# A fused attention and feed-forward kernel with its 522 operations in a new order

## The chip, the cores and the metric

The kernel runs on one core of a Trainium2 chip. A core has five engines with an instruction queue each: TensorE (PE in the profile; PEld is its weight load), VectorE (DVE), ScalarE (ACT), GpSimd (POOL) and SyncE (SP), which here only issues DMA transfers. Each queue runs in order, and semaphores hold an instruction until what it reads is there. TensorE writes to PSUM, which has eight banks of 512 float32 columns on 128 partitions; GpSimd does not touch PSUM in this kernel. The metric is the time of one execution on the device, in microseconds. A change of less than about 2% cannot be told from none.

## The reference

Two blocks are computed one after the other. Sizes are 4 batches, 4 heads, 1088 tokens, 32 features per head, 8 sketch rows.

```python
def phi(x):                                   # 64 features per token
    a = np.einsum('rd,bhsd->bhsr', S1, x)
    b = np.einsum('rd,bhsd->bhsr', S2, x)
    return np.einsum('bhsi,bhsj->bhsij', a, b).reshape(*x.shape[:-1], r * r)
q_p, k_p = (phi(q), phi(k))
kv = np.einsum('bhsf,bhsd->bhfd', k_p, v)
z = np.sum(k_p, axis=2)
num = np.einsum('bhsf,bhfd->bhsd', q_p, kv)
den = np.einsum('bhsf,bhf->bhs', q_p, z)[..., None] + 1e-06
attn = num / den
# heads side by side: x has 128 features per token
xn = (x - mu) / np.sqrt(var + 1e-06) * g_ln
out = x + np.maximum(xn @ w_ch1, 0.0) @ w_ch2
```

The sketches and both weights come as float64; the kernel turns them into float32 by itself, from their bits.

## The kernel before

The whole schedule is one list of operations, `PROGRAM` (lines 824 to 908), which is written out and run from top to bottom. The framework's own scheduling is off (`tc.manual_schedule()`), so each engine's queue holds its operations in the order of this list. Semaphores are derived from what the operations read and write. An operation is a name with arguments: the engine, where there is a choice (`V` VectorE, `A` ScalarE, `G` GpSimd, `S` SyncE), the batch or token chunk, a range, and the PSUM banks.

The work goes through these steps.

- *Fills* (`fill n w z`, line 247) multiply ones by ones into bank z; nobody reads the result.
- *Unpacking of weights* (`w_ex`, `w_bits`, `w_exf`, `w_mant`, `w_low`, `w_e2`, `w_e3`, `w_add`, `w_mul`, lines 274 to 336) makes float32 out of float64 for the sketches (0), the first weight (1) and the second (2). `fold` (352) takes the mean and the gain of the normalization into the first weight; `fold_cp` copies it out of PSUM.
- *Sketches*: `s_heads`, `sk`, `sk_0`, `sk_2`, `sk_8`, `sk_d` (lines 338 to 405) build the matrices by which tokens are multiplied.
- *Keys of a batch*: `turn_g`, `turn_r` (414, 424) transpose 32 by 32 blocks on VectorE. Batch 0 uses `k_dir` (448) with `k_cp` and `k_prod0`; the others use `k_feat` (466), `k_tok` (475), `k_prod`. Then come `k_sum` (490), `k_zs`, `k_sc`, `k_sccp` for the sum over tokens, `k_val` (519) for the product with the values, and `k_vcp`, `k_spr` (534), `k_rcp`, which lay it out.
- *Queries of a batch*: batch 0 is transposed on TensorE (`turn_p` 431, `turn_c`) and multiplied by `q_dir` (554); the others use `turn_g`, `q_feat` (587), `q_tok` (596). Then `q_ac`, `q_den`, `q_rec` make the reciprocal denominator, `q_a2` and `q_prod` the features, `q_turn` (634) turns them, and `num` (648) multiplies. `num_cp` and `num_r` copy the result to `xT`, one chunk of 512 tokens per half batch. The last 64 tokens of two batches form the narrow chunks 8 and 9.
- *Feed-forward of a chunk c*: `hid z c j t0 t1` (757) makes 128 of 512 hidden features for the 128-token tiles t0 to t1, `relu` (765 on ScalarE, 767 on VectorE) takes them to `hT`, and `sec z c t` (773) multiplies tile t by the second weight. There are two `hT` tiles, used in turn by the chunks in the order 0, 1, 2, 3, 8, 4, 5, 6, 7, 9.
- *Rows of a chunk*: `row_turn` (710), `row_wr` (716) and `row_rd` (722) bring the attention result to rows through DRAM (`row_pe`, `row_cp` for chunks 8 and 9). `st_bn`, `st_ag`, `st_pow` (730 to 743) make the normalization's factor. `fin` (786) scales and adds on VectorE; `fin_a` (791) scales on ScalarE, and `fin_g` (801) adds. `store` (807) and `store_r` (817) write to DRAM.

The loads are `ld` (121) for k and q rows, `ld_v` (129), `ld_vr` (135), `ld_t` (143) and `ld_tr` (150) for q of batch 0, `ld_w` (158), `ld_s` (112) and `ld_g` (116).

The four batches are interleaved: keys of the next batches run while `hid` and `sec` of the first chunks are worked through. A bank is free for its next writer when its readers are done, so the banks in the list decide whom a product waits for.

Of the kernel before, what the change touches and what calls it, by code (L numbers as in the profile page):

```python
# [25 lines left out]
def kernel(  # L26
# [810 lines left out]
    w_add G 1 0 256; k_dir 0 6 9 1; sk_2 4; k_prod0 3 6 6 3; w_mul G 1 0 256; turn_p 3 4 8;
    k_cp A 0 6 9 1; ld_v S 0 3; turn_c A 5 8 9; k_sum 0 7; sk_d 4; k_prod G 0 6 9; turn_c A 3 4 8;
    k_zs 0 7; turn_g k 1 0 4; k_sc 0 7; fold 3 0 256; k_sccp A 0 7; q_dir 4 9 2;
    fold_cp A 3 0 256; turn_r k 1; ld_v S 0 2; w_low A 2 0 512; w_bits V 2 0 512; w_ex V 2 0 512;  # L840
    ld_t S 2 0 4; k_feat 1 4 5; q_cp A 4 9 2 0 24; ld_t S 1 0 4; fill 1 512 1; w_exf A 2 0 512;
    k_tok 1 4 5; q_ac G 0 4 9; ld S k 2 0 34; w_mant A 2 0 512; c_vpad 2; q_den 0 4 9;
    ld S q 1 0 34; k_sum 1 7; q_rec 0 4 9; fold 3 256 512; w_e2 V 2 0 512; ld_v S 1 1;
    q_a2 V 0 4 9; ld_v S 1 2; w_e3 V 2 0 512; k_val 0 0 3 6; q_prod V 0 6 9; q_prod G 0 4 6;
    k_val 0 3 6 6; k_val 0 6 9 6; turn_p 2 0 4; k_zs 1 7; k_vcp A 0 6; k_prod G 1 0 5; q_turn 4 9;
    k_sc 1 7; turn_c A 2 0 4; k_spr 0 6; fold_cp A 3 256 512; q_dir 0 4 1; k_rcp A 0 6;
    k_sccp V 1 7; turn_g k 2 0 4; num 0 4 9 4 5 2 3; q_cp A 0 4 1 0 24; q_ac G 0 0 4; turn_r k 2;
    w_add G 2 0 512; q_den 0 0 4; k_feat 2 6 7; num_cp A 0 1 4 8 2 3; num_cp V 0 0 4 8 4 5;
# [1 line left out]
    k_tok 2 6 7; row_wr S 1; num_r A 0 4 5; hid 0 1 1 0 4; relu A 1 1 3 0 4; ld S q 2 0 34;  # L850
    turn_r q 1; turn_g q 1 0 4; q_prod G 0 0 2; ld_vr S 1 0; hid 7 1 2 0 4; relu A 0 1 1 0 4;
    k_sum 2 6; q_turn 2 4; w_mul G 2 0 512; relu A 7 1 2 0 4; row_rd S 1; q_feat 1 3 4 0 1;
    ld_v S 1 0; k_zs 2 6; q_turn 0 2; hid 7 1 0 0 4; ld_v S 1 3; k_prod G 1 5 9; q_tok 1 0 3 4;
    ld_vr S 2 0; k_sc 2 6; ld_vr S 1 1; relu A 7 1 0 0 4; num 0 0 4 4 5 2 3; k_sccp V 2 6;
# [1 line left out]
    num_cp A 0 1 0 4 2 3; q_den 1 0 4; sec 0 1 2; q_rec 1 0 4; st_bn 1; q_a2 G 1 0 4;
    q_prod G 1 0 4; sec 4 1 3; st_ag 1; row_turn 0 1 2 3; q_den 1 4 9; hid 6 0 1 2 4; q_rec 1 4 9;
    hid 3 0 3 0 2; q_a2 V 1 4 9; hid 0 0 0 0 2; relu A 3 0 3 0 2; row_turn 0 0 4 5; st_pow 1;
    k_val 1 0 9 2; relu A 6 0 1 2 4; q_turn 0 4; row_wr S 0; ld S k 3 0 34; sk_qq 3; fin_a 4 1 3;
    hid 5 0 0 2 4; q_prod G 1 4 9; turn_g q 2 0 4; relu A 0 0 0 0 2; hid 4 0 1 0 2; fin_a 0 1 2;  # L860
    hid 3 0 2 2 4; relu A 4 0 1 0 2; row_rd S 0; hid 6 0 2 0 2; k_vcp A 1 2; relu V 3 0 2 2 4;
    ld_v S 2 3; relu A 5 0 0 2 4; hid 0 0 3 2 4; turn_r q 2; relu A 6 0 2 0 2; ld S q 3 0 34;
    relu A 0 0 3 2 4; sec 3 0 2; sk_qq 2; q_turn 4 9; k_prod G 2 0 5; ld_v S 2 0; fin_a 7 1 0;
    ld_v S 3 1; q_feat 2 4 5 6 7; ld_v S 3 3; k_spr 1 2; q_tok 2 1 6 7; ld_v S 3 2; sec 3 0 1;
    k_rcp A 1 2; q_tok 2 0 4 5; k_prod G 2 5 9; num 1 0 9 1 2 6 7; st_bn 0; st_ag 0; sec 0 0 3;
    turn_r k 3; num_cp A 1 0 0 4 1 2; row_turn 3 1 6 7; st_pow 0; row_turn 2 1 6 7;
    num_cp V 1 0 4 8 1 2; sec 5 0 0; num_r A 1 6 7; num_cp A 1 1 0 4 6 7; turn_g k 3 0 4;
    fin_a 0 0 3; hid 4 2 3 0 4; fin_a 5 0 0; fin_a 3 0 1; fin_a 3 0 2; sec 0 1 1;
    num_cp A 1 1 4 8 6 7; fin_g V 0; row_turn 2 0 1 2; hid 3 2 0 0 4; fin_a 0 1 1; turn_r q 3;
    row_wr S 2; row_turn 3 0 1 2; fin_g G 1; row_pe 8 6; row_wr S 3; k_feat 3 0 1;  # L870
    relu A 3 2 0 0 4; row_cp V 8 6; ld_vr S 2 1; q_ac V 2 0 4; relu A 4 2 3 0 4; hid 2 2 2 0 4;
    ld_v S 2 2; q_ac G 2 4 9; ld_v S 2 1; q_den 2 0 4; k_tok 3 0 1; hid 3 3 2 0 4;
    relu A 2 2 2 0 4; q_rec 2 0 4; q_den 2 4 9; hid 4 3 0 0 4; row_rd S 3; relu A 3 3 2 0 4;
    q_rec 2 4 9; q_a2 V 2 0 4; row_rd S 2; turn_g q 3 0 4; q_prod G 2 0 4; k_sum 3 5; ld_vr S 3 0;
    hid 1 2 1 0 4; ld_vr S 3 1; k_zs 3 5; relu V 4 3 0 0 4; store S 0 0 4; hid 0 3 1 0 4;
    relu V 1 2 1 0 4; q_a2 G 2 4 9; k_sc 3 5; relu V 0 3 1 0 4; hid 4 3 3 0 4; q_prod G 2 4 9;
    st_bn 3; sec 3 2 2; st_bn 2; k_val 2 0 9 2; st_ag 2; k_sccp V 3 5; st_ag 3; q_feat 3 5 6 0 1;
    k_vcp A 2 2; st_pow 3; relu A 4 3 3 0 4; k_spr 2 2; q_tok 3 0 5 6; sec 7 3 3; k_rcp A 2 2;
# [64 lines left out]
```

## Time and profile before

| | |
|---|---|
| median of 3 runs | 105.92 us (105.67 to 109.9) |
| span of the profiled execution | 104.1 us |
| its time beside the span | not on the page |
| TensorE busy | 96.4 us |
| VectorE busy | 77.0 us |
| GpSimd busy | 54.4 us |
| ScalarE busy | 39.6 us |
| moved by DMA | 14.37 MB |

The page is one execution, seen by the hardware profiler. A group of instructions is named by its line, engine and operation, and by what it writes and reads. One float32 product is two matmul instructions, so `sec`, which is four products, is eight. Matmuls are pipelined, and the durations of neighbours overlap. A window row lists busy microseconds of PE, PEld, DVE, ACT and POOL, each with its count of instructions, then the granted clock of TensorE, the busy share of the DMA engines, and GB/s.

### The profile page before, as it was taken

The numbers are of one execution on the slowest core, as the hardware profiler recorded it, in microseconds if no ns is written. First come the engines' busy times: TensorE is split into PE (matmuls) and PEld (weight loads), VectorE is DVE, ScalarE is ACT, GpSimd is POOL, SyncE is SP. The second block draws the span as 40 slices with busy tenths as digits, with TensorE's granted clock in tenths as the row PEclk, the third lists the DMA queues.
The fourth block names the chain that finished last, engine by engine and source line by source line (L and its number), as shares of the span: only waits on it lengthen the run. The fifth ranks groups of instructions, "written<-read, shape, count | busy, mean of one in ns | idle before, by whom it ended". The sixth has DMA issues, their size and how long they took to land.

```text
span 104.1 us, 3156 instructions
## 1 busy us (share of the span) xinstructions
PE 96.4 (93%) x1271; PEld 68.3 (66%) x1271; DVE 77.0 (74%) x222; ACT 39.6 (38%) x96; POOL 54.4 (52%) x81
## 2 busy tenths in 40 slices
PE   4996989799999999999999999999999999999950
...
DVE  2899887999989976997985974999579271922430
...
GB/s 76 267 228 350 205 165 375 128 5 58 288 198 4 117 202 178 268 127 245 206 186 0 6 0 0 101 151 6 154 70 272 238 111 201 0 107 0 101 39 87
DMA packets 16991, 14.37 MB, mean 138 GB/s; under 512 B 6608, under 2 KB 13776, under 8 KB 16976
## 3 DMA queue, kind: packets, MB, share of 16 engines
...
q8 instruction: 10, 0.16, 0.7%
q10 hardware_dynamic: 112, 0.04, 0.2%
...
q0 software_dynamic: 32, 0.00, 0.0%
...
## 4 chain that ended last, share of the span: by engine, by line
PE 65%; DVE 20%; DMA 7%; issue 2%; ACT 2%; POOL 2%; POOLq 0%; DVEq 0%; ACTq 0%
PE ALL L757 27%; PE ALL L773 23%; PE ALL L648 4%; DMA xd<-xh 4%; DMA x<-xd 3%; PE ALL L519 2%; PE ALL L554 2%; DVE kp L87 2%; DVE qp L87 2%; DVE st L730 2%; PE ALL L587 1%; DVE xh L710 1%; PE ALL L466 1%; ACT xT L82 1%; DVE kT L414 1%
## 5 line engine op out<-in xcount | busy, mean ns | idle before, releaser
L773 PEld LDWEIGHTS ALL<-w,hT 128*128 128x128 f32 x272 | 32.6, 192 | 4.6 <-issue 4.1
L773 PE MATMUL ALL<-w,hT 128*128 128x128 f32 x272 | 33.8, 276 | 0.0
L757 PE MATMUL ALL<-xT,w 128*128 128x512 f32 (+1 forms) x72 | 31.7, 559 | 0.2
L765 ACT ACTIVATE hT<-ALL 128x512 f32<-128x512 f32 (+2 forms) x35 | 16.7, 500 | 22.7 <-PE ALL L757 17.0
L757 PEld LDWEIGHTS ALL<-xT,w 128*128 128x128 f32 x72 | 12.1, 190 | 7.6 <-issue 5.2
L87 POOL TENSOR_TENSOR qp<-a,fq 128x512 f32<-128x512 f32 (+2 forms) x7 | 12.2, 1745 | 3.1 <-DVE a L87 2.9
L87 POOL TENSOR_TENSOR kp<-kf 128x1280 f32<-128x1280 f32 (+2 forms) x6 | 13.2, 2211 | 0.0
L634 DVE STREAM_TRANSPOSE qpT<-qp 128x1280 f32<-128x1280 f32 (+2 forms) x9 | 10.9, 1225 | 0.2 <-POOL qp L87 0.2
L741 POOL TENSOR_TENSOR va<-mv,eps 128x4 f32<-128x4 f32 (+1 forms) x10 | 2.1, 206 | 17.1 <-DVE mv L736 17.1
L786 DVE SCALAR_TENSOR_TENSOR ob<-ALL,rstd,x 128x128 f32<-128x128 f32 x12 | 4.0, 347 | 8.3 <-PE ALL L773 7.2
L743 POOL TENSOR_TENSOR rstd<-va,mhalf 128x4 f32<-128x4 f32 (+1 forms) x10 | 9.3, 926 | 0.8
L767 DVE TENSOR_SCALAR hT<-ALL 128x512 f32<-128x512 f32 (+2 forms) x9 | 5.1, 571 | 5.6 <-PE ALL L757 5.6
L247 PE MATMUL ALL<-ones 128*128 128x512 f32 (+1 forms) x14 | 7.7, 688 | 1.5 <-DVE ones L190 1.5
L791 ACT ACTIVATE ob<-ALL,rstd 128x128 f32<-128x128 f32 x20 | 6.6, 368 | 5.9 <-PE ALL L773 2.8
L82 ACT COPY xT<-ALL 128x256 f32<-128x256 f32 x10 | 6.2, 640 | 5.9 <-PE ALL L648 4.3
L710 DVE STREAM_TRANSPOSE xh<-ALL 128x256 f32<-128x256 f32 x16 | 6.4, 421 | 1.2 <-PE ALL L648 0.8
L648 PE MATMUL ALL<-qpT,kvr 32*32 32x288 f32 (+2 forms) x320 | 7.2, 364 | 0.1
L730 DVE BATCH_NORM_STATS2 st<-x 128x6 f32<-128x128 f32 x32 | 6.7, 275 | 0.3 <-DMA x<-xd 0.3
L801 POOL TENSOR_TENSOR ob<-ob,x 128x512 f32<-128x512 f32 x3 | 3.9, 1296 | 5.4 <-ACT ob L791 5.4
L596 DVE STREAM_TRANSPOSE fq<-ALL 128x576 f32<-128x576 f32 x6 | 4.5, 768 | 1.6 <-PE ALL L587 1.6
L247 PEld LDWEIGHTS ALL<-ones 128*128 128x128 f32 x14 | 3.4, 268 | 3.4 <-issue 1.5
L87 POOL TENSOR_TENSOR ac<-fq 128x160 f32<-128x160 f32 (+1 forms) x6 | 3.1, 528 | 4.6 <-DVE fq L596 2.7
...
## 6 DMA issues: line engine op xcount, KB each, us to landing
vn<-in_v_dram SPq DMA_DIRECT2D x16, 128.0 KB, 5.6
...
```

The lines of the kernel that those rows point to most:

```text
L82: act.copy(o, i)
L87: by[eng].tensor_tensor(out=o, in0=a, in1=b, op=ALU.mult)
L247: pe.matmul(bank(z, 0, w), ones[:, 0:P], ones[:, 0:w], start=True, stop=True)
L634: dve.transpose(_ap(qpT, 0, P, 32 * u0, [[32, u1 - u0], [TW, 8], [1, 32]]), qp[:, H * F * u0 : H * F * u1])
L648: pe.matmul(bank(z[r], o, o + w)[D * h : D * h + D], kvr[b % 2][rows, DM * f + D * h : DM * f + D * h + D], qpT[rows, c : c + w], start=(f ...
L710: dve.transpose(_ap(xh[slot(c)], 0, P, 64 * n * i, [[32 * n, 2], [32, n], [1, 32]]), pair(z, P * (c % 2), [[32, n], [1, 32]]))
L730: dve.bn_stats(out=sts[slot(c)][:, 6 * t : 6 * t + 6], in_=row_ap(c, t))
L743: pool.tensor_tensor(out=rstds[slot(c)][:, 0:n], in0=vas[slot(c)][:, 0:n], in1=mhalf[:, 0:n], op=ALU.pow)
L757: pe.matmul(bank(z, 0, n), w1[:, P * j : P * (j + 1)], cols(c)[:, a : a + n], start=True, stop=True)
L765: act.activation(o, i, AF.Relu)
L773: pe.matmul(bank(z, DM * t, DM * (t + 1)), h[:, 512 * j + P * t : 512 * j + P * (t + 1)], w2[:, DM * j : DM * (j + 1)], start=(j == 0), st ...
L791: act.activation(ob(c)[:, P * t : P * (t + 1)], bank(z, P * t, P * (t + 1)), AF.Copy, scale=rstds[slot(c)][:, t : t + 1])
```

## The change

Only the list is changed. The computation stays: of the 522 operations all are there again, and three fills of 256 columns are added (7 before, 10 after; "operation" here means an entry of the list). The order is new on every engine, and most pieces have other PSUM banks. Some entries also change their engine:

- from GpSimd to VectorE: `w_add` and `w_mul` of the second weight, `q_ac` of batch 0 (tiles 4 to 9), of 2 (4 to 9) and of 3, and `k_prod` of batch 0 (6 to 9); `q_ac` of batch 1 and 2 (tiles 0 to 4) go from VectorE to GpSimd. `k_prod` of batch 3 is split the other way round.
- `q_a2` of tiles 0 to 4 goes to VectorE in batches 0, 1 and 3 and to GpSimd in batch 2; tiles 4 to 9 go to GpSimd in batch 0 and to VectorE in batch 2. `q_prod` goes to GpSimd in batch 0 (6 to 9) and 3 (0 to 4), to VectorE in batch 2 (4 to 9).
- from VectorE to ScalarE: the three `w_mant` of the sketches and the first weight, `row_cp` of both narrow chunks. `relu` and `num_cp` are dealt out anew between these two, with one more `num_cp` and `num_r` on VectorE.
- `store_r` of chunk 8 goes from SyncE's queue to ScalarE's.

All loads but the two sketches (ScalarE) and the gain (GpSimd) are issued by SyncE, as before, in a new order. The list's beginning, the stretch up to the first `sec`, and its end:

```diff
-    ld_w S 1 2 4; ld_s A 0; c_pads 1; c_small; c_ones; ld_g; c_act; ld S k 0 0 16; ld_s A 1;
-    fill 1 256 1; ld_w S 1 0 2; c_ac 0; c_vpad 1; c_vpad 0; ld_tr S; c_iota; c_ident;
-    fill 1 256 3; c_masks; ld_t S 3 4 8; c_vpad 3; fill 1 512 7; c_pads 0; ld S k 0 16 34; c_rest;
-    w_ex V 1 256 512; w_ex V 0 0 64; w_exf V 1 256 512; ld_t S 1 4 8; w_e2 V 1 256 512;
...
-    turn_g k 0 0 2; w_add G 1 256 512; ld_vr S 0 0; fill 1 512 2; sk_0 4; c_cg G; ld_t S 0 0 4;
-    turn_r k 0; turn_g k 0 2 4; ld_v S 0 1; sk_8 4; w_e2 V 1 0 256; k_dir 0 0 3 0; ld_v S 0 0;
...
-    q_rec 0 0 4; hid 1 1 3 0 4; q_a2 G 0 0 4; row_turn 1 0 4 5; row_turn 1 1 2 3; q_prod G 0 2 4;
...
-    q_tok 1 1 0 1; q_ac V 1 0 4; sec 7 1 0; num_cp V 0 0 0 4 4 5; q_ac G 1 4 9;
...
-    sec 0 7 1; fin 4 7 2; fin 1 7 3; store S 7 2 4; fin 0 7 1; store S 7 0 2;
+    ld_s A 1; c_pads 0; c_small; c_ones; c_vpad 0; c_ident; fill 1 256 6; fill 1 512 7; c_iota;
+    c_masks; fill 1 256 3; ld_s A 0; ld_w S 1 2 4; ld_t S 1 0 4; w_ex V 1 256 512; w_bits V 0 0 64;
+    c_ac 1; fill 1 512 3; fill 1 256 4; w_ex V 0 0 64; ld_g; w_exf V 1 256 512; ld_w S 1 0 2; w_mant
+    A 0 0 64; c_ac 0; w_exf V 0 0 64; w_low A 1 256 512; c_rest; w_e2 V 0 0 64; w_addlow V 0 0 64;
+    w_e3 V 0 0 64; w_bits V 1 256 512; ld S k 0 0 16; s_heads V; w_ex V 1 0 256; ld S k 0 16 34;
+    c_pads 1; turn_g k 0 0 2; w_bits V 1 0 256; sk 0; fill 1 512 7; turn_r k 0; sk_0 0; w_mant A 1 0
+    256; ld S k 1 0 34; ld_t S 0 0 4; fill 1 256 4; turn_g k 0 2 4; w_e2 V 1 256 512; ld_t S 2 0 4;
+    ld_t S 3 0 4; sk_q 0; c_vpad 1; w_exf A 1 0 256; w_e2 V 1 0 256; w_low A 1 0 256; w_e3 V 1 0
+    256; w_mant A 1 256 512; sk_2 0; k_dir 0 6 9 3; w_add G 1 256 512; ld_t S 1 4 8; ld_t S 3 4 8;
+    w_add G 1 0 256; w_mul G 1 0 256; c_cg G; sk_8 0; sk_d 0; ld_tr S; ld_t S 0 4 8; k_dir 0 0 3 4;
+    ld_t S 2 4 8; ld S k 2 0 34; ld_v S 0 1; k_cp A 0 0 3 4; k_dir 0 3 6 2; turn_g k 1 0 4; k_cp A 0
+    3 6 2; fill 1 512 1; ld_v S 0 3; turn_r k 1; ld_v S 0 0; k_cp A 0 6 9 3; turn_p 3 0 4; ld_v S 0
+    2; turn_c A 3 0 4; ld_vr S 0 1; k_prod0 0 3 4 0; k_sum 0 0; k_feat 1 4 7; k_prod0 3 6 2 3; k_zs
+    0 0; k_sc 0 0; k_sccp A 0 0; ld_vr S 0 0; w_e3 V 1 256 512; turn_p 5 8 9; turn_p 1 4 8; k_prod V
+    0 6 9; ld S q 1 0 34; turn_c A 1 4 8; q_dir 0 4 2; turn_c V 5 8 9; q_dir 4 9 1; q_cp A 0 4 2 0
...
+    0 4 9; q_rec 0 4 9; q_turn 0 2; fill 1 256 6; q_turn 2 4; k_rcp A 0 0; num 0 0 4 2 3 6 7; k_sccp
+    V 1 4; q_a2 G 0 4 9; k_zs 2 1; turn_g q 1 0 4; q_prod G 0 4 6; num_cp V 0 0 0 4 2 3; k_sc 2 0;
+    ld S k 3 0 34; fill 1 256 1; num_cp A 0 1 0 4 6 7; hid 1 0 0 0 2; row_turn 0 0 2 3; fold_cp A 4
+    256 512; hid 4 0 3 0 2; q_prod G 0 6 9; k_prod G 1 0 5; row_turn 0 1 6 7; relu A 4 0 3 0 2;
+    turn_r q 1; q_feat 1 6 7 2 3; relu A 1 0 0 0 2; ld_v S 1 3; q_turn 4 9; k_sccp V 2 0; hid 5 0 3
+    2 4; k_prod G 1 5 9; hid 1 0 2 0 2; q_tok 1 1 2 3; q_tok 1 0 6 7; relu A 5 0 3 2 4; q_ac G 1 4
+    9; relu V 1 0 2 0 2; ld_vr S 1 1; turn_g q 2 0 4; hid 0 0 1 0 2; relu V 0 0 1 0 2; q_den 1 4 9;
...
+    4; q_a2 V 1 4 9; hid 0 1 0 0 4; q_ac G 1 0 4; row_wr S 0; relu A 0 1 0 0 4; row_turn 1 1 4 5;
...
+    w_add V 2 0 512; ld S q 3 0 34; sk_qq 3; relu A 5 1 3 0 4; q_feat 2 2 3 6 7; k_feat 3 0 1;
+    row_rd S 1; k_spr 1 4; w_e3 V 2 0 512; w_mul V 2 0 512; sec 3 1 3; q_a2 V 1 0 4; ld_vr S 2 0;
...
+    st_pow 1; row_cp A 8 6; q_den 2 0 4; hid 6 8 2 0 1; hid 7 2 0 0 4; row_wr S 2; ld_v S 2 3; q_rec
...
+    2 0 4; q_prod V 3 4 9; row_rd S 4; hid 7 4 1 0 4; fin_a 4 3 0; hid 1 5 0 0 4; hid 4 5 3 0 4;
...
+    2; store S 6 0 4; store S 7 0 2; relu A 0 9 1 0 1; fin 1 7 3; store S 7 2 4; sec 0 9 0; fin 0
+    9 0; store_r S 9 0; store_r A 9 1;
```

More of the change, by code (lines that the diff above doesn't have):

```diff
@@ L837 @@
[L837 to L848, printed above, removed]
@@ L849 @@
-    q_rec 0 0 4; hid 1 1 3 0 4; q_a2 G 0 0 4; row_turn 1 0 4 5; row_turn 1 1 2 3; q_prod G 0 2 4;
[L850 to L854, printed above, removed]
@@ L855 @@
-    q_tok 1 1 0 1; q_ac V 1 0 4; sec 7 1 0; num_cp V 0 0 0 4 4 5; q_ac G 1 4 9;
[L856 to L878, printed above, removed]
@@ L879 @@
-    st_pow 2; q_turn 0 4; hid 5 8 2 0 1; sec 2 2 0; q_turn 4 9; hid 6 8 0 0 1; fin_a 2 2 0;
-    sec 7 3 2; relu A 5 8 2 0 1; q_tok 3 1 0 1; sec 6 2 3; q_ac G 3 0 4; hid 3 8 3 0 1;
-    relu A 6 8 0 0 1; num 2 0 9 4 5 1 2; q_ac G 3 4 9; fin_a 7 3 2; q_den 3 0 4; relu A 3 8 3 0 1;
-    st_bn 8; k_prod G 3 0 5; st_ag 8; hid 3 8 1 0 1; num_cp A 2 0 4 8 4 5; sec 7 3 0;
-    relu V 3 8 1 0 1; num_cp A 2 0 0 4 4 5; num_cp V 2 1 4 8 1 2; sec 0 2 1; row_turn 5 0 4 5;
-    num_cp A 2 1 0 4 1 2; st_pow 8; fin_a 7 3 3; row_turn 5 1 1 2; sec 3 8 0; num_r A 2 4 5;
@@ L885 @@
-    fin_a 7 3 0; q_den 3 4 9; row_wr S 5; fin_a 0 2 1; q_rec 3 0 4; q_rec 3 4 9; row_turn 4 0 4 5;
-    q_a2 G 3 0 4; hid 7 4 2 0 4; k_prod V 3 5 9; sec 5 3 1; row_turn 4 1 1 2; hid 0 4 0 0 4;
-    q_a2 V 3 4 9; row_wr S 4; relu A 7 4 2 0 4; q_prod V 3 0 4; ld_v S 3 0; fin_a 3 2 2;
-    hid 4 4 1 0 4; fin_a 6 2 3; fin_g G 2; q_turn 0 4; hid 1 5 2 0 4; hid 7 5 0 0 4;
-    q_prod V 3 4 9; relu A 1 5 2 0 4; relu A 4 4 1 0 4; k_val 3 0 9 5; fin 3 8 0; q_turn 4 9;
-    hid 4 5 1 0 4; fin_a 5 3 1; k_vcp A 3 5; store_r S 8 0; row_rd S 4; relu A 7 5 0 0 4;
```

72 lines of the change are left out of this document (50 added, 22 removed).

## The prediction

> **What bounds the kernel now.** I read the page first (shares, the span in slices), then the busy time by stage, then the chain in order of time, then the timeline of the head and the groups by form.
>
> ```profile
> PE 96.4 (93%) x1271; PEld 68.3 (66%) x1271; DVE 77.0 (74%) x222; ACT 39.6 (38%) x96; POOL 54.4 (52%) x81
> PE   4996989799999999999999999999999999999950
> DVE  2899887999989976997985974999579271922430
> ```
>
> ```profile
> 0.00:24.20 24.20, 20.30 (x279) 13.39 (x279) 20.12 (x58) 10.15 (x23) 14.73 (x37) 1.00 0.73 194
> 24.20:42.40 18.20, 18.13 (x351) 12.83 (x351) 16.31 (x39) 7.14 (x19) 16.98 (x16) 1.00 0.53 156
> 42.40:74.60 32.20, 32.12 (x417) 21.52 (x415) 26.47 (x67) 14.46 (x38) 15.93 (x18) 1.00 0.35 104
> 74.60:100.50 25.90, 25.80 (x228) 20.56 (x227) 13.81 (x60) 7.85 (x18) 6.79 (x11) 1.00 0.37 125
> ```
>
> The columns after the stretch are busy microseconds of PE, its weight load, DVE, ACT and POOL. From 24.2 us on TensorE is never idle, up to the last product. Before 24.2 it looks busy too, but much of that is fills and pipeline time, while VectorE works 20.1 of 24.2 us. So there are two stages: a head paced by VectorE, and a body paced by TensorE in which VectorE is close behind (16.3 of 18.2 us up to 42.4).
>
> The chain prices TensorE's pieces without the pipeline's overlap:
>
> ```profile
> 24.27 2.83 PE ALL L757 x6
> ...
> 46.50 0.86 PE ALL L757 x2
> ...
> 55.09 1.14 PE ALL L519 x72
> 56.23 0.71 PE ALL L587 x32
> ...
> 57.31 0.89 PE ALL L773 x8
> ...
> 61.60 1.53 PE ALL L648 x63
> ...
> 76.23 1.06 PE ALL L757 x2
> ...
> 100.44 0.35 DVE ob L786
> ```
>
> A full `hid` is 0.86, a `sec` 0.89, a whole `num` 1.53, a `k_val` 1.14, a `q_feat` 0.71; a `hid` behind products on 32 rows costs 0.2 more (1.06). Priced so, 32 full and 8 narrow `hid` are 29, 34 `sec` 30, `num` 7, and the smaller pieces of attention about 18: 84 us besides the fills. It ends at 100.4, so 16 us were lost: 13 before the first `hid` (24.27) and 3 behind it. Only these 16 can change, since the products are the same.
>
> **The change part by part.** No product is removed and three fills come. What moves is the order, some whole instructions between engines, and the PSUM bank of each piece.
>
> *Head, to the first k_dir.* GpSimd's `c_iota` releases the masks on VectorE.
>
> ```profile
> 0.72 0.15 POOL kT L226
> 1.28 0.79 POOL g_raw L116
> 1.38 1.28 ACT L199 ACT_TABLE_LOAD   x1 [1.38 <-PEq L927]
> 2.69 0.14 POOL row L203
> 2.86 0.22 DVE L214 TENSOR_SCALAR bit<-row 128x4 int32<-128x4 int32 x1 [1.41 <-POOL row L203]
> 6.33 0.41 DVE L87 TENSOR_TENSOR s_f<-mant,bits 8x256 f32<-8x256 f32 x1
> 9.70 1.55 PE L448 MATMUL ALL<-sk,kT 128*128 128x64 f32 x12 [1.00 <-DVE kT L414]
> 1.50 4.84 PE L247 MATMUL ALL<-ones 128*128 128x256 f32 x8 [1.50 <-DVE ones L190]
> ```
>
> In the new order `ld_g` (0.79) stands behind the iota, but `c_ident` ahead of it: masks at 2.3 instead of 2.86 (estimate). From there to `s_heads` took 3.47 us; two short steps leave this stretch (`w_mant` 0 goes to ScalarE, `w_e2` 1 moves back), 0.4 us, so `s_f` is ready at 5.8 to 6.0. Two more `w_mant`, one of which took 0.8, leave the way to `turn_g k 0`: kT is complete at 8.1. But behind `sk` TensorE now has a 512 and a 256 fill, 1.3 us at the `hid` rate, so `k_dir` starts at 8.2, against 9.70: gain 1.5. The five fills ahead of `sk` are 1792 columns where eight instructions (four fills, 1536) took 4.84 us; they end at about 6.2 and cost 0.2 at most. `c_act`, which brought the table load (1.28), now stands far behind; the load then falls to ScalarE's first `w_mant`, whose data come no earlier than 3.5, so it is hidden; without that cover it would cost 1.3 there.
>
> *Head, to the first hid.* VectorE now does more before the value path goes on:
>
> ```profile
> 13.15 0.20 DVE zT L498
> ```
>
> ```profile
> L87 DVE TENSOR_TENSOR kp<-ALL,kf 128x768 f32<-128x768 f32 x2 | 1.9, 953 | 0.4 <-ACT kf L82 0.4
> L414 DVE STREAM_TRANSPOSE kT<-kn 128x1024 f32<-128x1024 f32 x3 | 3.7, 1228 | 0.0
> L634 DVE STREAM_TRANSPOSE qpT<-qp 128x1280 f32<-128x1280 f32 x4 | 6.0, 1498 | 0.2 <-POOL qp L87 0.2
> L596 DVE STREAM_TRANSPOSE fq<-ALL 128x576 f32<-128x576 f32 x6 | 4.5, 768 | 1.6 <-PE ALL L587 1.6
> ```
>
> Behind kT (8.1) come six short steps (1.6), `turn_g k 1` and its rest (1.4), two `k_prod0` (1.9): `k_zs 0` ends at 13.1, against 13.35 (0.20 from 13.15). Most of the gain is spent on turning k of batch 1 early. Then VectorE has to the second `q_turn` 7.9 us: `w_e3` 0.4, `k_prod` 0.9, `turn_c` 0.2, two `k_tok` 1.5, `turn k 2` 1.4, two denominators with their two products 1.9, `k_zs` 0.2, two halves of `q_turn` 1.4. So `num 0` starts at 21.1. Ahead of its copy stand `k_sccp`, `k_zs` (0.3) and `turn_g q 1` (1.2), the copy is 0.6: the first `hid` at 23.2, gain 1.1 over 24.27.
>
> *Body, to num 1.* Here VectorE gets the unpacking of w2 whole (`w_add` and `w_mul` come from GpSimd).
>
> ```profile
> L310 DVE SCALAR_TENSOR_TENSOR bits<-w_raw,ex 128x512 uint32<-128x512 uint32 x1 | 0.7, 685 | 0.0
> L801 DVE TENSOR_TENSOR ob<-ob,x 128x512 f32<-128x512 f32 x2 | 1.4, 684 | 0.2 <-ACT ob L791 0.2
> L710 DVE STREAM_TRANSPOSE xh<-ALL 128x256 f32<-128x256 f32 x16 | 6.4, 421 | 1.2 <-PE ALL L648 0.8 <-ACT xT L82 0.5
> L765 ACT ACTIVATE hT<-ALL 128x512 f32<-128x512 f32 x22 | 12.7, 598 | 16.1 <-PE ALL L757 13.0 <-PE ALL L773 2.0 <-issue 1.1
> ```
>
> The first `sec` needs `w_mul 2`. From 23.2 VectorE has ahead of it: four `row_turn` 1.6, `turn` of q 2 and k 3 with three rests 3.0, `q_turn` 1.5, two `q_tok` 1.5, three half `relu` 1.2, denominators 1.5, `k_sccp` and `num_r` 0.4, w2 3.2 (three short steps and three of 0.68): 13.8 us, so 37.0. TensorE has 11.6 us of products ahead of that `sec`; it waits 2.1 us in all: 0.5 at `hid 0 1 0`, whose new bank is freed by a `relu` that stands in VectorE's queue behind two `q_tok` and `turn_g q 2`, 1.1 at `q_feat 2` for `turn_r q 2`, 0.5 at the `sec`. Behind it, five `sec` (4.45) and `num 1` (1.53) end at 43.0, against 42.4 at a comparable point: gain spent.
>
> *Body, from num 1 to the end.* TensorE's remaining products are 55.5 us by the prices above (24 full and 8 narrow `hid` 22.4, 29 `sec` 25.9, two `num` 3.1, two `k_val` 2.3, the rest 1.8). Before they were 56.1, with one `k_feat` more, and took 58.0 (42.4 to 100.4): 1.9 of switches and waits, which I keep. I add 0.7 for waits which the old order does not have: `hid 6 8 2` behind `row_cp`, now on ScalarE behind two copies (0.4), and `hid 4 5 3`, whose bank is freed behind a `relu` (0.6) that has to wait for `sec 4 3 0` (0.3). `num 3` then starts at about 76.1 instead of 74.6, with 1.5 us less of products behind it. VectorE carries 3.2 us more in all and GpSimd 5.5 less, but the last `q_turn` is ready 0.9 ahead of `num 3`, so this costs nothing while it stays under that. Last product 43.0 + 55.5 + 1.9 + 0.7 = 101.1.
>
> *The loads* keep their sizes and SyncE issues them all; k of batch 0 goes ahead of the q pieces.
>
> ```profile
> SPq L129 <- DMA w_raw<-in_moe_w_ch_dram: 1.5, 1, 1.5
> out_dram<-ob SPq DMA_DIRECT2D x2, 128.0 KB, 2.1
> out_dram<-ob SPq DMA_DIRECT2D x3, 32.0 KB, 1.9
> ```
>
> SyncE already waited once for an old load to land. I take nothing for them; the bounds are -0.5 (v early) and +3 (rival D). *The tail:* a last `fin` of 0.35 and two stores of 32 KB instead of one of 128 KB, 1.9 against 2.1 us: before, the span ended 3.3 us behind the last `fin`; I take 3.2.
>
> **Sum.** 101.1 + 0.35 + 3.2 = 104.7 us of span, against 104.1. The page gives no time beside its span; the median, 105.92, lies 1.8 above it. 104.7 + 1.8 = 106.5 us.
>
> **The rivals.**
>
> A, the forecast: the gain in the head is paid back in VectorE's queue; 106.5.
>
> B, faster: TensorE does not wait in the body. For it: VectorE starts its next instruction up to 0.1 before the last one's end, so 13.8 may be 12.8, and GpSimd is freed by 5.5 us. Against it: VectorE is given more just where it paces. Price: 23.2 + 73.1 of products + 1.5 of switches = 97.8, + 3.55 + 1.8 = 103.2. It decides once waits and switches behind 23.2 are under 2.0 us.
>
> C, slower: VectorE's products meet GpSimd's.
>
> ```profile
> 18.23 1.39 POOL L87 TENSOR_TENSOR qp<-a,fq 128x512 f32<-128x512 f32 x1 [1.34 <-DVE a L87]
> 18.60 1.83 DVE L87 TENSOR_TENSOR qp<-a,fq 128x768 f32<-128x768 f32 x1
> 70.46 1.45 DVE L87 TENSOR_TENSOR qp<-a,fq 128x1280 f32<-128x1280 f32 x1
> ```
>
> Alone, 1280 columns took 1.45, so 768 would take 0.87; beside GpSimd they took 1.83: 0.96 lost, about the 1.02 for which GpSimd was still running. In the new order VectorE has three such products beside GpSimd work (`k_prod V 0 6 9`, `q_prod V 2 4 9`, `k_prod V 3 0 5`) and `w_add` and `w_mul`: three times 0.96 and about 0.6, 3.5 us, of which 0.9 is slack: 109.1. It decides from 1 us on. The Trainium skill (SBUF — State Buffer, "Who interferes with whom") makes a rule of this: a VectorE instruction with two SBUF inputs and a GpSimd instruction that reads SBUF block one another for the whole instruction. By that rule the loss is up to GpSimd's whole instruction each time; the trace agrees with it at 18.60.
>
> D, slower: the late v and k 2 loads, now behind all q pieces, land up to 3 us behind need, and `k_val 0` and all behind it shift: 2 to 3 us, 108.5 to 109.5.
>
> **How the numbers follow.** A 0.50, B 0.24, C 0.16, D 0.10. The predicted time is A's, 106.5. A's own range is 104.5 to 108.0. The range 103.0 to 109.3 takes in the prices of all four and leaves out, with their own spread, 2 in 10. A measurement of this kernel tells 2% from no change, 103.8 to 108.0: faster 0.24, same 0.50, slower 0.26.
>
> **What would show it.** Right: `k_dir` near 8.2, first `hid` near 23.2, then a TensorE wait of about 2 us that VectorE ends (`turn_r q 2`, `w_mul`), `num 3` near 76. Wrong: a first `hid` beyond 24.3 (D), VectorE products of 1.8 us and more (C), or TensorE gapless from 23.2 (B).

## The result, and the profile after

The changed kernel takes 104.28 us, median of four executions (104.16 to 108.22), beside 105.80 for the kernel before on the same chip. The ratio is 0.986, 95% interval 0.984 to 0.988: 1.4% faster. In a later run of both kernels (after2 below) the ratio was 0.985 (0.980 to 0.990). The forecast was 106.5, slower by half a per cent; the time lies inside its range, but on the other side of the kernel before. That it lies in the range says little, since the range took in the prices of all four rivals. Executions near 108 us (near 110 of the kernel before) had a mean granted clock of 0.98 (0.95), and the ratios leave them out. The profiled execution after took 104.19 us, of which 102.4 are the span, again 1.8 less.

The page after: busy time, then PE and VectorE in 40 slices.

```profile
PE 95.9 (94%) x1277; PEld 68.8 (67%) x1277; DVE 78.2 (76%) x228; ACT 39.1 (38%) x96; POOL 48.4 (47%) x75
...
PE   4999999499999999999999999999999999999950
...
DVE  3868998869999999895999994997449367277330
```

The busy time by stage, columns as before the change, with the third border where `num 3` starts:

```profile
0.00:24.20 24.20, 21.38 (x306) 14.88 (x306) 18.91 (x58) 8.87 (x22) 13.51 (x37) 1.00 0.90 228
24.20:42.40 18.20, 18.20 (x352) 12.30 (x354) 17.68 (x43) 7.50 (x17) 12.51 (x10) 1.00 0.59 163
42.40:73.80 31.40, 31.40 (x402) 21.53 (x401) 26.70 (x68) 15.86 (x43) 14.81 (x17) 1.00 0.31 99
73.80:98.80 25.00, 24.94 (x226) 20.11 (x225) 14.56 (x62) 6.83 (x15) 7.52 (x13) 1.00 0.29 100
```

The DMA engines are busy for 0.90 of the head; before it was 0.73. From 24.2 to 42.4 TensorE has no gap at all, although VectorE is busier there than before (17.68 against 16.31). All the waits that the profile finds for TensorE, with the sum, the count and the longest:

```profile
PE ALL L247 <- DVE ones L190: 1.5, 1, 1.5
PE ALL L519 <- DMA vn<-in_v_dram: 1.3, 1, 1.3
```

The first is the start of the kernel. The second is `k_val 0`, which waits for v. The chain in order of time shows the same:

```profile
2.68 5.42 DMA kn<-in_k_dram
...
13.40 6.02 DMA vn<-in_v_dram
...
19.55 1.20 PE ALL L519 x70
...
24.26 1.02 PE ALL L757 x4
...
36.42 4.47 PE ALL L773 x40
40.88 1.53 PE ALL L648 x63
...
73.96 1.53 PE ALL L648 x63
...
98.78 0.35 DVE ob L786
```

The head is now a chain of loads (k until 8.10, v until 19.42). The first `hid` comes at 24.26 in the chain, which counts a piece from the end of the one ahead of it, and at 24.15 in the timeline; before, both gave 24.27. `num 1` runs at the same time as before. The whole gain lies behind it: the last product ends at 98.78 instead of 100.44.

To follow where time goes, the table gives the starts of the first `hid`, of `num 1` and of the last matmul in the profiled execution of every kernel of this study.

| kernel | first hid | num 1 | last matmul | hid to num 1 | num 1 to last |
|---|---|---|---|---|---|
| before | 24.27 | 40.82 | 100.13 | 16.55 | 59.31 |
| after | 24.15 | 40.81 | 98.47 | 16.66 | 57.66 |
| after2 | 24.18 | 40.83 | 98.49 | 16.65 | 57.66 |
| v_more | 24.33 | 43.85 | 101.50 | 19.52 | 57.65 |
| v_less | 25.06 | 42.66 | 100.32 | 17.60 | 57.66 |
| no_k2 | 22.88 | 43.89 | 101.54 | 21.01 | 57.65 |
| no_k23 | 22.54 | 42.65 | 100.31 | 20.11 | 57.66 |
| k2_later | 23.34 | 43.88 | 101.53 | 20.54 | 57.65 |
| switches | 24.43 | 43.27 | 102.07 | 18.84 | 58.80 |
| no_fills | 28.99 | 45.62 | 103.28 | 16.63 | 57.66 |
| shift | 36.26 | 52.91 | 110.57 | 16.65 | 57.66 |
| v_first | 24.24 | 45.67 | 103.33 | 21.43 | 57.66 |
| h1 | 24.25 | 40.78 | 105.79 | 16.53 | 65.01 |
| h2 | 24.97 | 41.63 | 105.69 | 16.66 | 64.06 |

Behind `num 1` the new order takes 57.66 us in every kernel that leaves it alone, to 0.01 us, whatever comes ahead. So that stretch is TensorE's own stream: other engines reach it at other times, and it does not change. Between the first `hid` and `num 1` it takes 16.65 wherever nothing was disturbed, even with heads of 29 and 36 us.

### The profile page after: what moved, and what is told of

It is laid out like the page before. It is cut to its first block, busy times and chain, and to the rows that moved or that the text cites. A ratio compares the mean times of both kernels' runs of the same rounds, so it can differ in the third digit from the quotient of the medians.

```text
span 102.4 us, 3171 instructions
## 1 busy us (share of the span) xinstructions
PE 95.9 (94%) x1277; PEld 68.8 (67%) x1277; DVE 78.2 (76%) x228; ACT 39.1 (38%) x96; POOL 48.4 (47%) x75
## 4 chain that ended last, share of the span: by engine, by line
PE 77%; DMA 11%; DVE 4%; SPq 3%; issue 1%
PE ALL L773 30%; PE ALL L757 29%; PE ALL L648 7%; DMA vn<-in_v_dram 6%; DMA kn<-in_k_dram 5%; PE ALL L519 5%; PE ALL L587 2%; DVE kT L414 2%; SPq L129 1%; PE ALL L247 1%; PE ALL L534 1%; SPq L158 1%; SPq L121 1%; PE ALL L466 1%; PE ALL L352 1%
## 5 line engine op out<-in xcount | busy, mean ns | idle before, releaser
L773 PE MATMUL ALL<-w,hT 128*128 128x128 f32 x272 | 33.2, 276 | 0.0
L757 PE MATMUL ALL<-xT,w 128*128 128x512 f32 (+1 forms) x72 | 30.5, 551 | 0.0
L87 POOL TENSOR_TENSOR qp<-a,fq 128x512 f32<-128x512 f32 (+3 forms) x8 | 12.9, 1619 | 13.5 <-DVE a L87 13.4
L87 POOL TENSOR_TENSOR kp<-kf 128x1024 f32<-128x1024 f32 (+1 forms) x5 | 10.6, 2121 | 3.9 <-PE ALL L519 3.9
L247 PE MATMUL ALL<-ones 128*128 128x256 f32 (+1 forms) x20 | 9.5, 614 | 1.5 <-DVE ones L190 1.5
L82 ACT COPY xT<-ALL 128x256 f32<-128x256 f32 x9 | 5.2, 638 | 11.9 <-PE ALL L648 10.7
L247 PEld LDWEIGHTS ALL<-ones 128*128 128x128 f32 x20 | 4.6, 251 | 4.2 <-issue 2.3
L519 PEld LDWEIGHTS ALL<-kp,vn 128*32 128x32 f32 x288 | 4.2, 110 | 3.8 <-issue 3.0
L519 PE MATMUL ALL<-kp,vn 128*32 128x64 f32 x288 | 4.8, 220 | 1.3 <-DMA vn<-in_v_dram 1.3
L648 PEld LDWEIGHTS ALL<-qpT,kvr 32*32 32x32 f32 x320 | 3.9, 103 | 2.6 <-issue 1.1
```

The lines of the kernel that those rows point to most:

```text
L87: by[eng].tensor_tensor(out=o, in0=a, in1=b, op=ALU.mult)
L247: pe.matmul(bank(z, 0, w), ones[:, 0:P], ones[:, 0:w], start=True, stop=True)
L519: pe.matmul(bank(z, 0, F)[D * h : D * h + D], vn[b][:, TW * h + D * u : TW * h + D * (u + 1)], kp[:, H * F * u + F * h : H * F * u + F * ( ...
L648: pe.matmul(bank(z[r], o, o + w)[D * h : D * h + D], kvr[b % 2][rows, DM * f + D * h : DM * f + D * h + D], qpT[rows, c : c + w], start=(f ...
L757: pe.matmul(bank(z, 0, n), w1[:, P * j : P * (j + 1)], cols(c)[:, a : a + n], start=True, stop=True)
L773: pe.matmul(bank(z, DM * t, DM * (t + 1)), h[:, 512 * j + P * t : 512 * j + P * (t + 1)], w2[:, DM * j : DM * (j + 1)], start=(j == 0), st ...
```

## The experiments

Two theories stood against each other. N: the gain lies behind `num 1`, in fewer changes between kinds of product, shorter waits, and work done earlier; the head is held by loads, and the body is TensorE's own work. The forecast's theory: VectorE's list sets when the first `sec` and `num 1` start, and takes back what the head gains. The word "after" in the expectations is the changed kernel.

**h1 and h2: the two orders joined at num 1.** h1 is the order of before up to and with `num 1`, then what is left in the order of after. h2 is the reverse. Banks of the second half are renamed to fit.

```diff
 h1:  k_prod G 2 5 9; num 1 0 9 1 2 6 7;
-     st_bn 0; st_ag 0; sec 0 0 3; turn_r k 3; num_cp A 1 0 0 4 1 2; ...
+     ld_vr S 3 0; ld_v S 2 1; turn_g k 3 0 4; ld_v S 2 2; turn_r k 3; k_feat 3 0 4; sec 3 0 3; ...
 h2:  q_ac G 2 0 4; num 1 0 9 3 4 0 2;
-     num_cp A 1 1 0 4 0 2; st_bn 0; k_prod G 2 5 9; num_r A 1 0 2; st_ag 0; k_sum 3 7; ...
+     c_vpad 3; c_vpad 2; sec 5 1 0; st_bn 1; st_ag 1; st_pow 1; fin_a 3 1 3; fin_a 5 1 2; ...
```

> The order of before up to and with num 1, then the order of after. Both kernels end num 1 at 42.4 us. Theory N (the gain lies behind num 1: fewer switches between kinds of product and shorter waits): 55.5 us of products, 0.66 for the k_feat 3 that this head hasn't done, and the 0.95 us of excess that after shows there: last product at 99.5 instead of 100.4, 104.8 us, 1.0% under before. Rival R (the gain is what the new head brings, its loads, engines and work done early): no change against before, 105.8.

> The order of after up to and with num 1, then the order of before. N: 42.4 + 55.5 + the 1.9 us of excess that before shows there = 99.8 for the last product, 0.6 under before: 105.2 us, and 0.9 above after. R: as after, 104.2.

Measured: h1 115.95, its best execution 111.52; h2 111.35, ratio 1.041 (1.033 to 1.048). Both expectations fail, by 5 us and more, and both behind the seam. What TensorE waits for in h1:

```profile
PE ALL L757 <- ACT xT L82: 2.7, 1, 2.7
...
PE ALL L773 <- DVE kf L475: 0.9, 1, 0.9
PE ALL L534 <- DVE xT L84: 0.9, 1, 0.9
```

After had turned k of batch 3 long before `num 1`; in h1 that turn, `k_feat 3` and `k_tok 3` come behind it, and a `sec` waits for their bank. A half of such an order presumes what the other engines did in the other half. The pair doesn't tell N from its rival. The table's last column compares whole orders: the tail of after keeps its 57.66 us behind heads with fewer loads and other engines, so these are not what shortens it. Work done early is in every one of these heads, and of that part N and R say the same.

**v_more and v_less: VectorE's list up to the first sec, longer and shorter.**

```diff
 v_more:
-w_mant A 2 0 512; w_exf A 2 0 512; q_ac G 1 4 9; q_ac G 1 0 4;
+w_mant V 2 0 512; w_exf V 2 0 512; q_ac V 1 4 9; q_ac V 1 0 4;
 v_less:
-w_add V 2 0 512; w_mul V 2 0 512;
+w_add G 2 0 512; w_mul G 2 0 512;
```

> After with w_exf and w_mant of w2 and both q_ac of batch 1 moved to VectorE: its list up to w_mul grows by about 1.4 us (0.4, 0.4, 0.3, 0.3), from 12.05 to 13.4. N: in after w_mul ends 0.25 ahead of the first sec, so now TensorE waits about 1.1 us there, and the span grows by 0.9 to 1.2: 105.1 to 105.4. If VectorE's list had slack that I don't see, no change: 104.2. If it paced already, the whole 1.4: 105.6.

> After with w_add and w_mul of w2 on GpSimd, as before had them: VectorE's list up to the first sec is 1.38 us shorter, and GpSimd, idle from 33.3 to 36.3, takes 2.6. The forecast's theory (VectorE's list sets when the first sec and num 1 start): 0.7 us or more faster than after. N (TensorE reaches the first sec by its own work): within 0.2 us of after's 104.2; num 1 at 40.9 as in after.

Measured: v_more 107.92, ratio to before 1.018 (1.014 to 1.023), 3.6 us above after (3.0 in the profiled execution) where 0.9 to 1.2 was expected. In order: TensorE's wait, the instruction of VectorE that made it so long, and GpSimd's beside it.

```profile
PE ALL L587 <- DVE qT L424: 2.3, 1, 2.3
```

```profile
31.71 2.33 DVE L296 TENSOR_SCALAR mant<-bits 128x512 f32<-128x512 uint32 x1
...
34.85 0.40 DVE L287 TENSOR_SCALAR exf<-ex 128x512 f32<-128x512 uint32 x1
```

```profile
31.37 2.39 POOL L87 TENSOR_TENSOR qp<-a,fq 128x1280 f32<-128x1280 f32 x1 [3.64 <-DVE a L87]
```

`w_mant` took 2.33 us, where `w_exf` of the same shape took 0.40: it ended 0.3 behind the GpSimd product that had begun 0.3 before it. So `turn_r q 2` ended 3.3 us later than in after, not 1.4, and the wait is at `q_feat 2` for that turn, the place that the forecast had named, with only some 0.2 us at the first `sec`. In after `turn_r q 2` ends at 33.89 and `q_feat 2` starts at 34.58: the order had 0.7 us in hand there.

v_less: 105.25, ratio 0.993 (0.988 to 0.998): no gain against after, a loss if anything. Its head came 0.9 later, because loads landed later (the turn of k of batch 0 started at 7.80 us, in after at 6.55), and the first `sec` waited:

```profile
PE ALL L773 <- POOL w L87: 0.7, 1, 0.7
```

VectorE's list was 1.4 us shorter and nothing came sooner. But the test is weaker than meant. GpSimd ended `w_mul` at 37.94, and the first `sec` went on at 37.99, so another engine had become the bound; and what left VectorE stands behind `turn_r q 2`, so `q_feat 2` could not gain (it lies 10.43 us behind the first `hid` in both kernels). That VectorE doesn't set the pace in after rests on after's own trace, in which TensorE waits nowhere from the first `hid` to `num 1`. How close it is to doing so, v_more shows.

**no_k2 and no_k23: a head with fewer loads.**

```diff
 no_k2, no_k23:
-ld S k 2 0 34;
 no_k23 alone:
-ld S k 3 0 34;
```

> After without the load of k for batch 2 (544 KB, issued ahead of the v pieces of batch 0); batch 2 is then computed with the k of batch 0, which still lies in its buffer. TensorE's 1.3 us of waiting for v before k_val 0 should go: num 0 at 21.1 instead of 22.3, first hid at 22.9 to 23.2. N (the head is held by the loads and the body is TensorE's own work): the whole of it reaches the end, 1.0 to 1.3 us under after, 102.9 to 103.2. The forecast's theory (a head that is faster is paid back in VectorE's queue): first hid as early, but TensorE waits about as much at q_feat 2 or the first sec, 104.2. If v doesn't come sooner without those 544 KB, first hid stays at 24.2 and 104.2.

> After without the loads of k for batches 2 and 3 (2 x 544 KB; those batches are computed with the k of batches 0 and 1, which lie in their buffers). Theory L (the block of instructions waits behind bulk loads): without k 3, issued at 20.3 us, the block comes at 22 to 24 us, TensorE doesn't stand still at the 705th record, and the head's gain of no_k2 (first hid 22.9 instead of 24.2) reaches the end: 102.9 to 103.2. Rival (the stall comes with any head that is faster, whatever is loaded): a stall of 1.8 to 2.5 us between 25 and 29 us again and 104.2 or more. The forecast's theory (VectorE's queue takes the gain back): no stall there, but a wait of 0.5 us or more at q_feat 2 or the first sec.

Measured: no_k2 106.3, ratio 0.987 (0.978 to 0.996); no_k23 103.52, ratio 0.972 (0.967 to 0.976), its best executions 102.68 and 102.76. TensorE in no_k2: `k_val 0`, the first `hid`, and `hid 0 0 1`:

```profile
18.16 1.21 PE L519 MATMUL ALL<-kp,vn 128*32 128x64 f32 x72
...
22.88 1.12 PE L757 MATMUL ALL<-xT,w 128*128 128x256 f32 x4
...
28.27 0.59 PE L757 MATMUL ALL<-xT,w 128*128 128x256 f32 x2 [2.51 <-DVE qT L414]
```

Without those 544 KB `k_val 0` starts at 18.16 without a wait, and the first `hid` at 22.88, the forecast's 23.2 and a little better. So the loads held the head. By how much differs between executions with the same loads: `k_val 0` started at 19.55 in after, at 18.30 in k2_later and at 20.45 in v_less. The gain didn't reach the end of this execution: a stall of 2.5 us followed, and then the clock fell for 3.4 us (last section); the best execution, 104.21, is no better than after. In no_k23 the profiled execution has the same stall (1.7), but the two best executions lie 1.5 to 1.6 us below after's median, about the 1.6 by which its first `hid` comes sooner; three more lie 0.4 to 1.3 below and have no trace. The profiled execution has no wait at `q_feat 2` or at the first `sec`, though its stall gave VectorE more time; and 102.7 leaves room for a few tenths of one at most. The forecast's theory, which asked for 0.5 us or more there, falls.

**switches: three more changes between kinds of product behind num 1, one ahead of it.**

```diff
-k_sum 3 7; ... sec 6 0 2; ...           k_val 3 0 9 0; sec 5 3 1; ...
+sec 6 0 2; k_sum 3 7; ...               sec 5 3 1; k_val 3 0 9 0; ...
-k_val 2 0 9 1; q_feat 3 5 7 0 2; hid 4 8 1 0 1; ...   hid 0 1 1 0 4; ... k_val 1 0 9 4;
+k_val 2 0 9 1; hid 4 8 1 0 1; q_feat 3 5 7 0 2; ...   k_val 1 0 9 4; hid 0 1 1 0 4; ...
```

> After with four pieces exchanged with a neighbour so that four more changes between 128-row products and products on 32 rows or columns occur (k_sum 3 and k_val 3 each one place later, hid 4 8 1 one place earlier, k_val 1 one place earlier). N (a change there and back costs about 0.2 us): + 0.6 to 0.9 us against after, 104.8 to 105.1, with no new wait for another engine. Rival (a change costs nothing, what before lost there were waits): 104.2.

Measured: 106.6, ratio 1.001 (0.996 to 1.005), by the ratios 1.6 us above after, more than expected; the best execution was 105.36, 1.2 above the best of after (104.16). The table has the clean number: `num 1` to the last matmul takes 58.80 instead of 57.66, 1.14 more. First after, then switches, around `num 2` and `k_val 3`:

```profile
61.25 1.60 PE L648 MATMUL ALL<-qpT,kvr 32*32 32x288 f32 x64
...
64.92 1.02 PE L757 MATMUL ALL<-xT,w 128*128 128x512 f32 x2
```

```profile
64.04 1.60 PE L648 MATMUL ALL<-qpT,kvr 32*32 32x288 f32 x64
...
68.42 1.12 PE L757 MATMUL ALL<-xT,w 128*128 128x512 f32 x2 [0.55 <-ACT kvc L82]
```

The same products take 4.38 instead of 3.67 us. 0.55 is a new wait (the `hid` needs the bank of `k_val 3`), 0.16 is the change there and back. The same reading gives 0.15 at `k_sum 3` and 0.17 at `k_val 2`. So a change there and back costs 0.16, not 0.2, and "costs nothing" falls too. The remaining 0.1 of the 1.14 is the `hid` behind the new wait, which took that much longer.

**k2_later: work of the head put behind the first hid.**

```diff
-k_sum 2 1; ... k_zs 2 1; ... k_sc 2 0; ... hid 1 0 0 0 2; ... q_feat 1 6 7 2 3;
+... hid 1 0 0 0 2; ... q_feat 1 6 7 2 3; k_sum 2 4; ... k_zs 2 4; ... hid 0 0 1 0 2; k_sc 2 6;
```

> After with k_sum 2, k_zs 2, k_sc 2 and its copy moved from the head to behind q_feat 1, where before had them. N (in the head TensorE does them in idle time, behind the first hid they cost their own time): + 0.4 to 0.6 us, 104.6 to 104.8, first hid still at 24.2. Rival (they weren't free in the head either): first hid 0.3 to 0.5 earlier, 104.2.

Measured: 106.62, ratio 1.000 (0.996 to 1.003), 1.4 us and more above after; the expected 0.4 to 0.6 can't be read from the time, because the stall came here as well. From the first `hid` to `num 1` it took 20.54; less 16.65, less the stall of 1.8 and 1.7 for 3.41 us at half clock, 0.4 are left. That is in line with the expectation, by a subtraction and no more. The first `hid` did not stay at 24.2, though: it came at 23.34. Most of this is v, which landed earlier in this execution: `k_val 0` was through 0.6 us sooner (19.96 instead of 20.56). From there to the first `hid` it took 3.38 instead of 3.59, so the moved products, about 0.5 us, were not quite free in the head, as the rival said: 0.2 of them counted.

**no_fills.**

```diff
-fill 1 512 7; ... fill 1 256 4; ... fill 1 512 1; ... fill 1 256 6; ... fill 1 256 1;   (behind sk)
```

> After without five of its fills: the last 512 x 7 ones behind sk, 256 x 4 behind turn_r k 0, 512 x 1, 256 x 6 and 256 x 1 ahead of the first hid. N: 104.2, within 0.2. If the fills hold TensorE up at k_dir or num 0: 0.3 or more faster. If the clock needs them: granted clock under 1.00 and 1 us or more slower.

Measured: 107.61 (104.95 to 109.66), with a mean clock of 0.93 to 0.95 in seven of eight executions. Stretches of its profiled execution, of which the middle one has half the clock (the column behind the counts):

```profile
5.20:8.60 3.40, 2.19 (x11) 1.27 (x9) 1.49 (x4) 0.51 (x1) 0.00 (x0) 1.00 0.98 283
8.60:22.30 13.70, 11.41 (x77) 9.74 (x78) 8.95 (x20) 4.10 (x12) 4.45 (x7) 0.50 0.88 199
22.30:40.00 17.70, 16.83 (x428) 10.89 (x427) 16.59 (x41) 9.01 (x21) 12.74 (x12) 1.00 0.63 166
```

The fills are work after all: without them the head's products run at half speed and the first `hid` comes at 28.99 (of the 4.8 us, 1.1 are there at `k_dir` already, which waited for kT until 10.26). The one execution at full clock (104.95) was not faster than after, so nothing shows that the fills hold TensorE up.

**after2 and v_first.** after2 is the changed kernel unaltered. v_first loads v of batch 0 ahead of k of batch 2 and moves what needs that k behind it:

```diff
-ld S k 2 0 34; ld_v S 0 1; ... ld_v S 0 3; ... ld_v S 0 0; ... ld_v S 0 2; ... ld_vr S 0 1; ... ld_vr S 0 0;
+ld_v S 0 1; ld_v S 0 3; ld_v S 0 0; ld_v S 0 2; ld_vr S 0 1; ld_vr S 0 0; ld S k 2 0 34;
-turn_r k 2; turn_g k 2 0 4; ... k_feat 2 3 6; k_tok 2 3 6; ... k_sum 2 1; ... num 0 0 4 2 3 6 7; ...
+... num 0 0 4 2 3 6 7; k_sccp V 1 4; turn_r k 2; turn_g k 2 0 4; ... num 0 4 9 2 3 4 5; k_feat 2 0 7; ...
```

> After once more, beside the next two on the same chip: 104.2. In the traces so far TensorE stood still for 1.8 to 2.5 us at one and the same place of its instruction stream (the 705th record) in no_k2, k2_later and switches, and not in after, v_more and v_less; the block of instructions that TensorE's queue loads there (16 KB) came at 25.8 to 26.6 us in the former and at 23.8 to 24.8 in the latter. If that is chance of an execution, some executions of after lie 1.8 to 2.5 us above the others at full clock; if it depends on v's loads being early, none does.

> After with the six v loads of batch 0 ahead of the k load of batch 2, and with what needs that k moved behind: its turns behind k_sccp 1 on VectorE, k_feat 2, k_tok 2, k_sum 2, k_zs 2 and k_sc 2 behind num 0's second half. Everything is computed. v should land by 17.5, k_val 0 start at 17.3 to 18.2, num 0 at 20 to 21, first hid at 21.8 to 22.9 (1.3 to 2.4 earlier); TensorE pays 1.2 us of products that move behind it, VectorE 2.3. L with TensorE as the bound: 103.0 to 104.0. The forecast's theory: q_feat 2 waits for turn_r q 2, 0.5 to 2 us, and 104.2 to 105. If the stall at the block of instructions comes: 105 to 106.

Measured: after2 104.72, ratio 0.985 (0.980 to 0.990), and its profile repeats that of after to 0.03 us; the stall isn't in it. Four of its six executions lie within 1.2 us of each other, the other two 3.8 and 4.7 us above the profiled one; those two had a lower mean clock (0.98) and have no trace, so it isn't shown that the stall never comes to after. v_first 108.82, ratio 1.017 (1.010 to 1.024). `k_val 0` started at 17.67, as meant, and `num 0` at 21.26; but the turn of k 2 now stands on VectorE ahead of the copy for which the first `hid` waits (1.3 us, first `hid` 24.24), `k_feat 2` and its followers cost two waits of about 1 us, and the clock was at half for 3.4 us as well. It isn't a better kernel.

**shift: no_k23 with 32 narrow fills more.**

```diff
 fill 1 512 3; fill 1 256 4;
+fill 32 16 7;
```

> no_k23 with 32 fills of 16 columns more ahead of sk (64 records of TensorE's stream, some 1 to 1.5 us in time in which it waits for s_f and kT anyway). In the profiled executions of no_k2, no_k23, k2_later and switches TensorE stood still at its 705th record, where its next block of instructions had landed 1.3 to 1.4 us before. If the block is the cause, the stall is again at record 705, now 64 records earlier in the order (at the first hid or q_feat 1, not at hid 0 0 1), or it falls into the wait for xT and there is none: 102.7 and a spread of less than 1 us between executions at full clock. If the instruction at that place waits for another engine (relu and turn of q 2 on VectorE), the stall stays at hid 0 0 1, record 769, and the times are those of no_k23, 102.7 to 103.9.

Measured: 116.04, ratio 1.095 (1.091 to 1.099). It missed its question. The narrow fills did not take 1 to 1.5 us: TensorE was at its fills until 18.08 us (the narrow ones took 11.3), the clock was at half from 9.38 to 23.03, so the first `hid` came at 36.26, long after the loads had landed. There was no stall at record 705, but nothing was left to collide with. What it shows is the 16.65 and 57.66 of the table once more.

## Why the prediction was wrong

**The head to the first hid (23.2): only the order of engines was costed, "I take nothing for" the loads.** The masks and the sketches came as forecast or sooner, and `k_zs 0` ended at 13.44 against 13.1. But `k_dir` started at 9.15, not 8.2, since kn landed at 8.10 and its turns stand behind that, and v landed at 19.42, when TensorE had waited 1.3 us. Rival D had this mechanism at 2 to 3 us. It was 1.0: 24.15 instead of 23.2. no_k2 and no_k23, with first `hid` at 22.88 and 22.54, show that it was the loads. The DMA share of the head, 0.73 before and 0.90 after, left little room for moving k 1 and all q pieces ahead of v.

**The body to num 1: "13.8 us, so 37.0", and a wait of 2.1 us.** This is the first of two steps that turned the sign, and it failed by a mis-sized term. From the end of VectorE's half of `num_cp` to the end of `w_mul` 2 it took 12.05 us, not 13.8. Rows of VectorE's timeline after (start, duration):

```profile
23.32 0.64 DVE L84 COPY xT<-ALL 128x256 f32<-128x256 f32 x1
...
26.17 1.45 DVE L596 STREAM_TRANSPOSE fq<-ALL 128x576 f32<-128x576 f32 x2
27.54 0.39 DVE L767 TENSOR_SCALAR hT<-ALL 128x256 f32<-128x256 f32 x1
27.85 1.23 DVE L414 STREAM_TRANSPOSE qT<-qn 128x1024 f32<-128x1024 f32 x1
29.00 0.39 DVE L767 TENSOR_SCALAR hT<-ALL 128x256 f32<-128x256 f32 x1
...
33.65 0.24 DVE L424 STREAM_TRANSPOSE qT<-qn 128x64 f32<-128x64 f32 x1
33.89 0.69 DVE L315 TENSOR_TENSOR mant<-mant,low 128x512 f32<-128x512 f32 x1
...
35.32 0.69 DVE L87 TENSOR_TENSOR w<-mant,bits 128x512 f32<-128x512 f32 x1
```

Most start before the one above has ended: 27.54 against 26.17 + 1.45 = 27.62, 29.00 against 27.85 + 1.23 = 29.08. A list in which nothing waits advances by start to start, some 0.08 us less for most instructions, and over the 27 of this stretch that is 1.9 us. The forecast added durations, and gave the overlap only to rival B. TensorE's list was 12.1 us, not 11.6: it goes to products on 32 rows or columns and back three times, and three times 0.16, which the 11.6 leaves out, is the difference (an estimate, at the price that switches measured). So VectorE ended 0.25 us ahead of the first `sec`, and 0.7 ahead at `q_feat 2`. The mechanism itself is real and next in line: v_more brought it out at the very place. That it did not act in after is what the trace shows, and no_k23 agrees.

**Num 1 to the end: "1.9 of switches and waits, which I keep", and 0.7 added.** This is the second step that turned the sign. Forecast 58.1 us from the end of `num 1`, measured 56.4 (42.4 to 98.8): of the 1.9 only 0.9 came, of the 0.7 nothing. The two waits that were added, at `hid 6 8 2` and `hid 4 5 3`, are not in the trace, where TensorE waits nowhere behind the first `hid`. And the 1.9 was treated as a property of the kernel, while it is one of the order. Between starts of `num 1` and the last matmul after saves 1.65 us. 0.65 of it is `k_feat 3`, which now stands ahead of `num 1` (forecast, at 0.6). Before enters products on 32 rows or columns six times behind `num 1` (`k_feat 3`, `k_sum 3`, `k_val 2`, `num 2`, `k_val 3`, `num 3`), after three times, because `k_feat 3` is gone from there and `k_sum 3` and `k_val 3` stand next to others: three times 0.16 is 0.5, at the price that switches measured. Of the rest, 0.5, most is one wait. In the kernel before, the first `hid` behind `num 1` waits for a copy that ScalarE makes of attention results:

```profile
43.80 0.64 ACT L82 COPY xT<-ALL 128x256 f32<-128x256 f32 x1
...
44.49 0.30 PEld L757 LDWEIGHTS ALL<-xT,w 128*128 128x128 f32 x2 [0.27 <-ACT xT L82]
```

With the slower start behind it, this costs 0.35 us from start to start. In after, such a `hid` comes later, and TensorE waits for none. The last 0.15 is spread over small pieces. No experiment took this wait away by itself. The `k_feat 3` is paid for in the body, where `k_sum 2` and `k_sc 2` left for the head, which had time for most of them (0.4 behind the first `hid`, k2_later), and where the first `hid` is 0.1 earlier; so `num 1` starts at 40.8 in both kernels.

**Rival C: the products of VectorE and GpSimd collide.** The products that C named took 0.95 us (`k_prod` 0), 1.46 (`q_prod` 2) and 1.44 (`k_prod` 3), about what they take alone. For the last two, and for `w_add` and `w_mul`, GpSimd had nothing to do (33.3 to 36.3 us at the latter). The first, from 13.69 to 14.64, did meet a GpSimd product, and there GpSimd paid. The two halves of the first weight's `w_mul`, of one size:

```profile
11.39 0.73 POOL L87 TENSOR_TENSOR w1g<-mant,bits 128x256 f32<-128x256 f32 x1
...
13.86 1.37 POOL L87 TENSOR_TENSOR w1g<-mant,bits 128x256 f32<-128x256 f32 x1 [1.24 <-DVE bits L310]
```

The second, which began 0.17 us behind VectorE's product, took 0.64 more; nothing on the path waited for it. VectorE paid once as well: its small product at 54.84 (128x128) took 1.04 us beside GpSimd's addition, and TensorE did not wait. In v_more it was VectorE's `w_mant` that came second, and it paid. The Trainium skill (SBUF — State Buffer, "Who interferes with whom") says that whichever of the two issues first holds the shared ports for its whole instruction, and counts `tensor_scalar` in a two-port mode among VectorE's instructions that need them; these cases agree with it, though no run shows in which mode `w_mant` ran. So C's mechanism is there, and the new order placed it where it costs nothing.

**The balance.** Head + 0.95, the stretch from the first `hid` to the end of `num 1` - 1.55 (18.2 instead of 19.8), behind it - 1.7: 104.7 becomes 102.4. Either of the two gains alone would have brought the sum under the 104.1 of before, had the head come as forecast; with the head's loss either alone would have come out about even (104.1 and 103.95). Rival B had the body right and D the mechanism of the head. The condition that the forecast set for B, under 2.0 us of waits and switches behind the first `hid`, was met with about 1.5, which is what B itself had put down; its 103.2 missed by the head.
